# Issuing a 3.5 KB weight load from GpSimd three instructions earlier, ahead of the building of the head mask

## The chip, the cores and the metric

The kernel runs on one core of a Trainium2 chip. The metric is the device time of one execution in microseconds (us). The profile's span, from the first to the last instruction, is about 2.1 us shorter than the device time of the same execution. In the profile PE is TensorE's products, PEld its weight loads, DVE VectorE, ACT ScalarE, POOL GpSimd, and SPq, ACTq and POOLq are the queues on which SyncE, ScalarE and GpSimd issue transfers.

## The reference, cut to what matters

```python
# x [2048, 448], 16 heads of 28
qkv = x @ wqkv
pq = einsum("bhsd,hdf->bhsf", q, w_phi)      # a 28 x 28 matrix for each head
pk = einsum("bhsd,hdf->bhsf", k, w_phi)
phi = concat([softmax(p), softmax(-p)])      # for q and for k
# ... linear attention from phi_q, phi_k, v; output product with wo
b = gelu(x @ w1 + b1) @ w2 + b2
return g * a + (1 - g) * b                   # g = sigmoid(sum(x * gate_w))
```

The kernel multiplies the projections with w_phi once, ahead of everything that runs over tokens: Wpk = Wk times a block-diagonal matrix of the heads' w_phi, and Wpq in the same way. That block-diagonal matrix is what the moved load feeds.

## The kernel before

The parts that the argument touches. GpSimd builds an identity and a head mask, then issues the load of the last 64 rows of w_phi; ScalarE's queue loads the first 384.

```python
nc.scalar.dma_start(x0, x[0:512, :]...)                       # first block of x, 448 KB
nc.sync.dma_start(gate[0:1, :], gate_w[None, :])
for c, eng in ((0, nc.sync), (1, nc.scalar), (2, nc.sync)):   # WvG
    eng.dma_start(WvG[:, c, 0:D], A_wqkv[c * P:(c + 1) * P, 2 * D:3 * D])
nc.scalar.dma_start(WvG[64:P, 3, 0:D], ...)
nc.scalar.dma_start(wphi[:, 0:3, :], wphi_rows[0:384, :]...)  # the large w_phi load
# [cut]
load_wT(WkT, D)                                               # DMA transposes, SyncE
load_wT(WqT, 0)
# [cut]
nc.gpsimd.memset(ident[:], 1.0)
nc.gpsimd.affine_select(out=ident[:], ...)
nc.gpsimd.memset(hmask[:], 1.0)
nc.gpsimd.affine_select(out=hmask[:], ...)                    # twice
nc.gpsimd.dma_start(wphi[0:64, 3, :], wphi_rows[384:448, :])  # the small w_phi load
nc.gpsimd.memset(Wpq[0:HP, 3, :], 0.0)
# [cut: more clears on GpSimd]

def fill_bd():                                 # VectorE, four products, one for each chunk
    for c, (h0, h1) in enumerate(spans):
        nc.vector.tensor_tensor(out=bd[:, c, h0:h1, :], in0=wphi[:, c, ...],
                                in1=hmask[:, c, h0:h1, ...], op=ALU.mult)
# [cut]
dummies(7)            # TensorE: warm-up products
turn_x0(0, xp[0]); turn_gate(); turn_x0(1, xp[1])   # transposes of x on TensorE (L367)
fill_bd()
v_pair(0, on_act=True); v_pair(1)                   # 16 v products (L212)
prep(WkT, wk_at, (1, 0, 1)); prep(WqT, wq_at, (1, 0, 0))   # the weight products (L262)
swap_on_pool(WvS, WvG)                              # GpSimd copies (L400, L401), and others
# [cut: the k, q and v products over all tokens, the MLP, the output]
```

The softmax here doesn't subtract the row's maximum and nothing guards it: scores larger than these inputs give would overflow.

## Time and profile before

| | kernel before |
|---|---|
| device time, 3 runs | 149.19 us (149.14 to 149.22) |
| span of the profiled run | 147.5 us (that run: 149.62 us) |
| TensorE busy | 97% of the span |
| GpSimd busy | 46%, almost gapless to 12.5 us |
| the moved load | issued at 2.22 us, 0.76 us on GpSimd, landing after 4.2 us |

The lines of this profile are in the prediction, except one, the weight loads ahead of the second weight product, with their wait in brackets:

```profile
10.50 0.94 PEld L262 LDWEIGHTS <-WqT 128*128 128x128 bf16 x16 [0.46 <-DMA WqT<-in_A_wqkv_dram]
```

### The profile page before, as it was taken

How to read it: one execution, taken by the hardware profiler on the slowest of the kernel's cores; microseconds unless marked ns; L12 is line 12 of the kernel's file. 1: busy time of each engine (PE TensorE's matmuls, PEld its weight loads, DVE VectorE, ACT ScalarE, POOL GpSimd, SP SyncE). 2: the span in 40 equal slices, each digit the busy share in tenths (PEclk: the TensorE clock that was granted, in tenths of full speed). 3: DMA queues.
4: the chain of work that ended last, by engine and by line, in shares of the span. 5: the costliest groups of instructions: out<-in, count | busy, mean ns of one | idle time of the engine just before them, and what ended most of it. 6: DMA issues, size and time to landing. Idle time of an engine off the chain costs nothing.

```text
span 147.5 us, 3138 instructions
## 1 busy us (share of the span) xinstructions
PE 143.4 (97%) x1302; PEld 75.0 (51%) x1302; DVE 87.9 (60%) x139; ACT 75.2 (51%) x91; POOL 68.4 (46%) x49
## 2 busy tenths in 40 slices
PE   7999999999999999999999999999999999999992
PEld 2665544555544854444444445554555455555462
DVE  2353699999999999999300017765665245550312
ACT  1654999989889436767677774000621021111100
POOL 7999999899977999919950000000000000000000
PEclk9999999999999999999999999999999999999999
DMA  4999999999700089982999913333433012225011
GB/s 142 227 215 193 168 195 222 218 220 214 160 2 2 4 144 131 226 169 47 126 158 201 351 66 71 71 76 73 129 98 76 31 62 67 67 67 71 31 62 31
DMA packets 44928, 18.02 MB, mean 122 GB/s; under 512 B 36785, under 2 KB 44914, under 8 KB 44914
## 3 DMA queue, kind: packets, MB, share of 16 engines
q1 hardware_dynamic: 43698, 17.16, 56.5%
q10 hardware_dynamic: 1152, 0.65, 1.6%
q8 instruction: 10, 0.16, 0.5%
q14 instruction: 4, 0.03, 0.1%
q0 software_dynamic: 64, 0.01, 0.0%
HBM read 6.28 MB, written 1.84 MB: 55 GB/s over the span
## 4 chain that ended last, share of the span: by engine, by line
PE 91%; DMA 4%; SPq 2%; DVE 1%; issue 0%
PE y L515 29%; PE hp L463 29%; PE pq L346 7%; PE y L520 6%; DMA WqT<-in_A_wqkv_dram 4%; PE v_ps L330 4%; PE pk L338 4%; PE pk L231 3%; PE acc L353 3%; PE nm L476 3%; SPq L146 2%; PE v_ps L231 2%; PE y L525 1%; PE w_ps L262 1%; PE pk L218 1%; SPq L134 1%
## 5 line engine op out<-in xcount | busy, mean ns | idle before, releaser
L515 PE MATMUL y<-w_sb,gel 128*128 128x448 bf16 (+2 forms) x238 | 45.2, 342 | 0.0
L463 PE MATMUL hp<-xT,w_sb 64*128 64x512 bf16 x196 | 42.6, 376 | 0.0
L463 PE MATMUL hp<-xS,w_sb 64*128 64x512 bf16 x196 | 42.6, 376 | 0.0
L468 ACT ACTIVATE gel<-hp,b1T 128x1024 bf16<-128x1024 f32 x28 | 30.8, 1110 | 13.2 <-PE hp L463 13.2
L515 PEld LDWEIGHTS <-gel 128*128 128x128 bf16 x238 | 22.3, 98 | 20.0 <-issue 0.9
L538 ACT ACTIVATE b2u<-b_sb,ungate 128x448 f32<-128x448 bf16 x16 | 10.2, 666 | 40.8 <-DVE res L530 40.8
L463 PEld LDWEIGHTS <-w_sb 64*128 64x128 bf16 x392 | 19.0, 94 | 23.0
L306 POOL TENSOR_TENSOR phik<-phik,rec 128x1792 bf16<-128x1792 bf16 (+1 forms) x8 | 24.9, 3126 | 1.8 <-DVE rec L303 1.7
L480 DVE TENSOR_SCALAR den<-nm,einv 128x16 f32<-128x16 f32 x16 | 3.7, 230 | 27.9 <-PE nm L476 27.9
L530 DVE SCALAR_TENSOR_TENSOR res<-y,ungate,b2u 128x448 bf16<-128x448 f32 (+2 forms) x17 | 10.8, 653 | 15.4 <-PE y L525 10.1
L301 DVE TENSOR_REDUCE sums<-phik 128x64 f32<-128x1792 bf16 x8 | 16.0, 2000 | 3.2 <-ACT phik L292 3.2
L306 POOL TENSOR_TENSOR oT<-oT,rec 128x1792 bf16<-128x1792 bf16 x4 | 12.7, 3212 | 1.1 <-DVE rec L303 1.1
L520 PE MATMUL y<-wo_sb,oT 128*128 128x448 bf16 (+2 forms) x51 | 11.7, 341 | 0.0
L346 PE MATMUL pq<-Wpq,xT 64*128 64x448 bf16 x56 | 11.5, 349 | 0.0
L346 PE MATMUL pq<-WqS,xS 64*128 64x448 bf16 x56 | 11.4, 349 | 0.0
L306 POOL TENSOR_TENSOR w_sb<-w_sb,rec 128x1792 bf16<-128x1792 bf16 x3 | 9.6, 3212 | 3.0 <-DVE rec L303 3.0
L483 DVE TENSOR_TENSOR o_tok<-nm,den 128x448 bf16<-128x448 f32 x16 | 10.0, 624 | 0.6
L303 DVE RECIPROCAL rec<-sums 128x64 f32<-128x64 f32 x16 | 8.8, 553 | 1.4
L200 DVE CAST vaug<-v_ps 128x896 bf16<-128x896 f32 x7 | 7.5, 1071 | 2.0 <-PE v_ps L212 1.6
L291 ACT ACTIVATE phik<-pk 128x896 bf16<-128x896 f32 x8 | 7.6, 947 | 1.9 <-PE pk L220 1.9
L301 DVE TENSOR_REDUCE sums<-oT 128x64 f32<-128x1792 bf16 x4 | 7.9, 1981 | 0.0
L292 ACT ACTIVATE phik<-pk 128x896 bf16<-128x896 f32 x8 | 7.7, 958 | 0.0
(113 smaller groups left out, 173.6 us busy)
## 6 DMA issues: line engine op xcount, KB each, us to landing
w_sb<-in_B_w_dram SPq DMA_DIRECT2D x4, 784.0 KB, 11.5
out_dram<-res SPq DMA_DIRECT2D x15, 112.0 KB, 1.8
w_sb<-in_B_w_dram SPq DMA_DIRECT2D x2, 448.0 KB, 4.8
w_sb<-in_B_w_dram SPq DMA_DIRECT2D x2, 336.0 KB, 3.7
xS<-xT SPq DMA_DIRECT2D x2, 256.0 KB, 3.5
EqT<-in_A_x_dram ACTq DMA_DIRECT2D x1, 448.0 KB, 3.2
xS<-xT SPq DMA_DIRECT2D x2, 192.0 KB, 3.5
wo_sb<-in_A_wo_dram SPq DMA_DIRECT2D x1, 336.0 KB, 16.9
```

What stands on the lines that cost most here:

```text
L292: nc.scalar.activation(out=dst[:, :, :, 1, 0:PW], in_=src, func=ACT.Exp, scale=-1.0)
L301: nc.vector.reduce_sum(out=sums[:], in_=ph, axis=AX.X)
L303: nc.vector.reciprocal(out=rec[:], in_=sums[:])
L306: eng.tensor_tensor(out=ph[:, lo:hi], in0=ph[:, lo:hi], in1=rec[:, lo:hi, :, None].to_broadcast([P, hi - lo, 2, DH]), op=ALU.mult)
L346: nc.tensor.matmul(pq[:, i, 0:D], lhsT=x_half(i, k, h)[:, r * P:(r + 1) * P], rhs=w_half(Wpq, WqS, i, k), start=(k == 0), stop=(k == NK - 1))
L463: nc.tensor.matmul(hp[:, i, :], lhsT=w1_sb[i * HP:(i + 1) * HP, k, j * P:(j + 1) * P], rhs=x_half(i, k, h), start=(k == 0), stop=(k == NK ...
L468: nc.scalar.activation(out=gel[h][:, j, :], in_=hp[:].rearrange("p a b -> p (a b)"), func=ACT.Gelu_apprx_tanh, bias=b1T[:, j:j + 1])
L483: nc.vector.tensor_tensor(out=o_tok[:, t % 4, 0:D].rearrange("p (x h d) -> p x h d", x=NPR, h=2), in0=nmv[:, :, 0:PW].rearrange("p x (h d) ...
L515: nc.tensor.matmul(y, lhsT=gel[t // 8][:, j, (t % 8) * P:(t % 8 + 1) * P], rhs=w2_sb[:, j, cols], start=(opens and j == 0), stop=False)
L520: nc.tensor.matmul(y, lhsT=oT[:, c, t * P:(t + 1) * P], rhs=wo_sb[:, c, cols], start=False, stop=(closes and c == 2))
L530: nc.vector.scalar_tensor_tensor(out=res[:, cols], in0=y, scalar=ungate[:, t:t + 1], in1=b2u[t][:, cols], op0=ALU.mult, op1=ALU.add)
L538: nc.scalar.activation(out=b2u[t][:], in_=b2_sb[:], func=ACT.Copy, scale=ungate[:, t:t + 1])
```

## The change

Its intent is to bring the small load forward, since the idle time of VectorE in front of the block-diagonal matrix is put down to "wphi". Nothing else changes.

```diff
     nc.gpsimd.affine_select(out=ident[:], in_=ident[:], pattern=[[-1, P]],
                             compare_op=ALU.is_equal, fill=0.0, base=0, channel_multiplier=1)
+    nc.gpsimd.dma_start(wphi[0:64, 3, :], wphi_rows[384:448, :])
     nc.gpsimd.memset(hmask[:], 1.0)
     [cut: the two affine_select of hmask]
-    nc.gpsimd.dma_start(wphi[0:64, 3, :], wphi_rows[384:448, :])
     spans = [(0, 5), (4, 10), (9, 14), (13, 16)]
```

## The prediction

> **What bounds the kernel now.** I started with the page of the profiled execution, its busy shares and its chain of work that ended last.
>
> ```profile
> span 147.5 us, 3138 instructions
> ...
> PE 143.4 (97%) x1302; PEld 75.0 (51%) x1302; DVE 87.9 (60%) x139; ACT 75.2 (51%) x91; POOL 68.4 (46%) x49
> ...
> PE 91%; DMA 4%; SPq 2%; DVE 1%; issue 0%
> ```
>
> TensorE is busy 97% of the span and makes up 91% of the chain. GpSimd, the engine whose order changes, is busy 46% of the span and has no entry in the chain. The part that is not TensorE lies at the start, so I next took the chain in order of time. The columns are start in us, length in us, and what it was.
>
> ```profile
> 2.53 0.04 issue
> 2.58 2.37 SPq L146
> 4.94 0.05 issue
> 4.99 5.47 DMA WqT<-in_A_wqkv_dram
> 10.46 0.05 issue
> 10.51 1.10 PE w_ps L262 x16
> 11.61 2.27 PE pk L231 x12
> 13.88 0.29 PE pk L218
> ```
>
> The chain runs through the SyncE queue: it issues the DMA transpose for WkT (2.37 us), then the one for WqT at 4.99, which lands 5.47 us later, at 10.46. Then TensorE starts the second weight product at 10.51 and works without a gap to the end (the remaining pieces of the chain follow each other on TensorE to 144.8, then the last output). So a change in the first 10 us is worth something only if it moves the landing of WqT, and something ahead of TensorE's other work only if it comes later than its slack. The view of waits for TensorE says the same: over the whole kernel it waits 1.1 us for the zeroed warm-up tile and 0.3 us for WqT, and for nothing else that is listed.
>
> What the moved load feeds: the timeline of the first microseconds shows it, and the product that consumes it.
>
> ```profile
> 1.47 0.15 POOL L166 MEMSET hmask<- 128x64 bf16 x1
> 1.68 0.27 POOL L167 TENSOR_SCALAR_AFFINE_SELECT hmask<-hmask 128x64 bf16<-128x64 bf16 x1
> 2.02 0.25 POOL L169 TENSOR_SCALAR_AFFINE_SELECT hmask<-hmask 128x64 bf16<-128x64 bf16 x1
> 2.22 0.76 POOL L171 DMA_DIRECT2D wphi<-in_A_w_phi_dram  x1
> ...
> 6.85 0.92 DVE L191 TENSOR_TENSOR w_sb<-wphi,hmask 128x140 bf16<-128x140 bf16 x4 [0.99 <-DMA wphi<-in_A_w_phi_dram]
> ```
>
> VectorE builds the block-diagonal weights (called w_sb in the trace, bd in the code) from wphi and hmask in four instructions, and sat idle 0.99 us before the first, for a wphi load. There are two: the large one on ScalarE's queue (chunks 0 to 2) and the small one on GpSimd's (64 rows of chunk 3). The table of DMA issues tells which came last.
>
> ```profile
> wphi<-in_A_w_phi_dram ACTq DMA_DIRECT2D x1, 21.0 KB, 4.3
> wphi<-in_A_w_phi_dram POOLq DMA_DIRECT2D x1, 3.5 KB, 4.2
> ```
>
> The small load is issued at 2.22 and takes 4.2, so it lands at about 6.4. The large one is issued at 2.42 (timeline) and takes 4.3, so it lands at about 6.7. The first VectorE instruction multiplies chunk 0 and waits for the large load; only the fourth, which starts at 7.5 (the view of this tile gives the last start), reads the small one. The small load has 7.5 - 6.4 = 1.1 us to spare before its only reader, and it is not what the idle 0.99 us waited for.
>
> **What the Trainium skill says.** "DMA: Bandwidth & Descriptors", in "SWDGE vs HWDGE vs iDMA", says that a DMA issued from GpSimd has its descriptors written by software on that engine, into rings kept in SBUF. The trace agrees that issuing is not free there: this 64-row load holds GpSimd's queue for 0.76 us, the 14-row bias load later for 0.54 us. The same page, "Issuing engines are not separate DMA queues", says DMAs from all queues run on the same 16 engines and interleave. The trace shows GpSimd's queue with 64 packets in all and a share that rounds to 0.0% of the DMA engines' span, so as traffic it is negligible at either place. "SBUF — State Buffer", in the box on the "DVE blocks DMA" trap, says VectorE in a two-port mode can lock GpSimd out of the port it needs for descriptors. That is the only way I see for the new place to cost more: VectorE clears tiles from 0.90 to 2.19. In the kernel before, GpSimd's own memset and selects run beside these at 0.15 to 0.29 us each without a visible stall, but its descriptor writing begins at 2.22, after the last clear, so the trace before does not show this case either way.
>
> **The change part by part.** It removes and adds nothing. The order of instructions on TensorE, VectorE, ScalarE and SyncE is the same before and after, waits included; on GpSimd one DMA issue moves ahead of three instructions.
>
> - The small load: the three instructions it overtakes occupy GpSimd's stream from 1.47 to 2.22, so its issue moves up by 0.75 us, to about 1.47. It should land near 1.47 + 4.2 = 5.7 instead of 6.4. Its reader at 7.5 does not care. Gain on the path: 0.
> - The head mask: its three instructions start behind the 0.76 us issue, so hmask is complete at 2.27 + 0.76 = about 3.0 instead of 2.27. Its reader starts at 6.85, 3.8 us later. Loss on the path: 0.
> - GpSimd after that: the next instruction (the clear of Wpq) started at 2.97, behind 0.75 + 0.75 us of these four. The same four in another order add up to the same, so it should start at 2.97 again, within about 0.05 us for the switch between issuing and computing. Everything later on GpSimd keeps its time.
> - VectorE's build at 6.85 to 7.77 still waits for ScalarE's load at 6.7. And had it moved, nothing would follow: TensorE reaches its first use of the blocks at 8.93 to 9.12 (timeline), 1.2 us after they are complete, because it is busy with the first v products; and then waits for WqT at 10.46.
> - DMA traffic: 3.5 KB leave the window around 4.2 to 5.1 us and go to around 3.5 to 4.4 (from the packets' start times in the trace). Per packet record it is 16 data packets of 16 ns and 16 completions of 9 ns, 0.4 us of engine time over 16 engines: 0.025 us each. This sits at worst ahead of the x block that TensorE transposes at 4.09, and at best no longer ahead of WkT and WqT. Estimated from these: -0.03 to +0.03 us.
>
> The sum is 0 +- 0.05 us on 149.19.
>
> **The rivals.**
>
> 1. The head start reaches the end. The idle 0.99 us in front of VectorE's build reads as if it were for the moved load, since the profile names both loads wphi. If it were, the build could begin 0.7 us sooner. For it: only the name. Against it: the two landings (6.4 and 6.7), and WqT behind it; even a build that took no time would leave TensorE at WqT's landing. Time: 149.2 all the same; the most that taking away the wait for WqT gives is its 0.3 us, 148.9.
> 2. Descriptor writing collides with VectorE's clears. In the new place, 1.47 to 2.22, it lies beside the clears of WvG (1.52 to 1.95) and Wpk (1.95 to 2.19). If GpSimd could not write until 2.19, its stream would slip by up to 0.7 us. It is nearly gapless from 0.81 to 12.53 us, so the slip would travel to the copy of x that TensorE's k products need (12.78, 0.61 us long). That copy has 0.25 us of wait for a transpose ahead of it and ends at 13.39, some 0.4 us before TensorE gets to L218 at 13.81. So of 0.7 us about 0.05 could reach TensorE, and the copies of WqS have 0.7 us to spare as well (19.04 against 19.77). Time: 149.2 to 149.3; 149.6 only if the slip is twice that. A clear is one output and no input, so I give a stall as such one chance in five.
> 3. Rearranged DMA traffic moves WqT's landing. All 16 engines are busy at 90% or more in most slices from 2.5 to 12 us, so the order of packets can matter more than their size. For it: the transposes are the path. Against it: SyncE issues them back to back (2.58 to 7.60), and its order and waits are unchanged. If the landing shifted by 0.2 us either way, the time would be 149.0 to 149.4.
>
> **The range and the chances.** The three runs of the kernel before lie within 149.14 to 149.22, so repetition alone gives 0.1 us. I add 0.2 us either way for rival 3, and a little above for rival 2 and for another chip: 148.9 to 149.5, centred on 149.2. A change of 2% is 3.0 us; no path here gives a third of that: the whole of TensorE's waiting is 1.4 us. So within 2% gets 0.97, and the rest is split evenly.
>
> **What would show each step right or wrong.** In the changed kernel's timeline: the small load's issue at about 1.5 us and 0.75 us long (over 1 us, with hmask's clear late, would be rival 2); hmask complete by about 3.0; the clear of Wpq at about 3.0; VectorE's build still at about 6.85, still waiting for a wphi load although the small one landed at about 5.7; TensorE's first use of the blocks still at about 9.1; the landing of WqT within 0.2 us of 10.46, and the span within 0.3 us of 147.5. A build that starts at 6.1 would show that I took the wrong load for the last one; a WqT landing half a microsecond away would show rival 3. The prediction as a whole is wrong if the time leaves 148.9 to 149.5, most likely by the transposes' landing.

## The result, and the profile after

| | before, same rounds | changed |
|---|---|---|
| device time, 4 runs each | 149.20 us (149.14 to 149.24) | 149.16 us (149.03 to 149.31) |
| ratio | | 0.9998, 95% interval 0.998 to 1.0015 |

A ratio is the mean time of one kernel's fast runs over that of the other's fast runs of the same rounds, so it isn't quite the ratio of the medians.

The page of the changed kernel (its span, and the chain that ended last by engine):

```profile
span 147.0 us, 3138 instructions
...
PE 97%; DVE 1%; issue 0%
```

The span is 0.59 us shorter than in the profile of before (147.54 and 146.96), though the medians of the times are equal, and the DMA that had 4% of the chain is gone from it. The chain in order of time (start, length, what) shows what has taken its place:

```profile
1.06 3.17 PE warm_ps L384 x7
4.23 0.92 PE xp L367 x8
...
5.17 0.70 DVE xT L200
...
5.92 3.22 PE v_ps L212 x16
9.14 1.89 PE w_ps L262 x32
11.03 2.27 PE pk L231 x12
```

TensorE goes from its warm-up products through the transposes of x and the v products into the weight products, and no wait for WqT shows. It was close: WqT, issued at 5.00, landed at 9.86, and the first product that reads it started at 9.90. In the profile of before TensorE waited for that landing until 10.46. The timeline of GpSimd and VectorE shows the moved instruction and its reader:

```profile
1.49 0.76 POOL L166 DMA_DIRECT2D wphi<-in_A_w_phi_dram  x1
...
2.25 0.18 POOL L167 MEMSET hmask<- 128x64 bf16 x1
...
2.83 0.25 POOL L170 TENSOR_SCALAR_AFFINE_SELECT hmask<-hmask 128x64 bf16<-128x64 bf16 x1
3.03 0.46 POOL L173 MEMSET Wpq<- 64x448 bf16 x1
...
6.01 0.96 DVE L191 TENSOR_TENSOR w_sb<-wphi,hmask 128x140 bf16<-128x140 bf16 x4
```

The issue moved from 2.22 to 1.49 and is as long as before, the mask is complete at 3.08, and the clear of Wpq starts 0.06 us later than before. VectorE's build starts at 6.01, 0.84 us sooner than in the profile of before. The table of DMA issues (last column: us from issue to landing) says why:

```profile
wphi<-in_A_w_phi_dram ACTq DMA_DIRECT2D x1, 21.0 KB, 3.5
...
wphi<-in_A_w_phi_dram POOLq DMA_DIRECT2D x1, 3.5 KB, 3.5
```

Both w_phi loads are faster than in the profile of before, the large one too, which the change doesn't touch (4.3 before). So the two profiles differ in things that the diff doesn't explain. Are these differences the change's doing, lost again elsewhere, or are they of the single run? That was the first question for the chip.

### The profile page after: what moved, and what is told of

It reads as the page before. It is cut to its first block, busy times and chain, and to the rows that moved or that the text cites. A ratio compares the mean times of both kernels' runs of the same rounds, so it can differ in the third digit from the quotient of the medians.

```text
span 147.0 us, 3138 instructions
## 1 busy us (share of the span) xinstructions
PE 142.9 (97%) x1302; PEld 74.5 (51%) x1302; DVE 87.9 (60%) x139; ACT 75.2 (51%) x91; POOL 68.4 (47%) x49
## 3 DMA queue, kind: packets, MB, share of 16 engines
HBM read 6.28 MB, written 1.84 MB: 55 GB/s over the span
## 4 chain that ended last, share of the span: by engine, by line
PE 97%; DVE 1%; issue 0%
PE y L515 29%; PE hp L463 29%; PE pq L346 7%; PE y L520 6%; PE v_ps L330 4%; PE pk L338 4%; PE pk L231 3%; PE acc L353 3%; PE nm L476 3%; PE v_ps L212 2%; PE warm_ps L384 2%; PE v_ps L231 2%; PE w_ps L262 1%; PE y L525 1%; PE xp L367 1%; PE pk L218 1%
```

## The experiments

Theory: the position of this load is worth nothing, and what differs between the two profiles differs from run to run. Rival: the earlier load brings the other transfers, and with them WqT, forward by half a microsecond. Eleven runs were made, in three calls; the kernels of one call ran on the same chip and share the runs of the kernel before (medians 149.39, 149.10 and 149.31 us).

### Both kernels again, twice each

No edit.

> The kernel before, unchanged, a second time. Theory: the landing of the WqT transpose and the end of TensorE's slow start differ from run to run, whatever the kernel, so the 0.5 us between the two first profiles (147.5 and 147.0) is such a difference. Then the ratio of this kernel to before is 1.000 with an interval of about 0.1 to 0.2%, and its WqT may land anywhere from 9.6 to 10.6. Rival (the moved load brings WqT forward): WqT lands at 10.4 to 10.5 again, the span is 147.5 again.

> The changed kernel a second time, timed on the same chip as the repeat of before. Theory: ratio 1.000, within 0.1%; WqT anywhere from 9.6 to 10.6. Rival: WqT lands at 9.9 or sooner again, span 147.0 again, and the ratio is 0.997 or lower.

> A third profile of the kernel before. Theory: the landings of WqT in the profiles of before and of the changed kernel overlap. Rival: all those of before lie at least 0.3 us later than all those of the changed kernel.

> A third profile of the changed kernel. Theory: as for the third profile of before, the landings overlap; GpSimd's issue at 1.5 and the clear of Wpq at 3.0 repeat to 0.05 us. Rival: WqT at 9.9 or sooner in all three.

Measured: before_rep1 149.22 us (148.90 to 149.50, 6 runs), ratio 0.9988 (0.9969 to 1.0007); after_rep1 149.29 us (148.99 to 149.41, 6 runs), ratio 0.9993 (0.9977 to 1.0009); before_rep2 149.17 and after_rep2 149.68 us, one run each. All six profiles together (the last column is from the trace's record of the granted clock: the moment from which TensorE has its full clock):

| profile | device us | span us | w_phi landings, small / large: us from issue | WqT issue + landing | v products, us | build starts | full clock from |
|---|---|---|---|---|---|---|---|
| before | 149.62 | 147.5 | 4.2 / 4.3 | 4.99 + 5.5 | 3.37 | 6.85 | 6.26 |
| before_rep1 | 149.47 | 147.4 | 3.6 / 3.6 | 4.90 + 4.8 | 3.60 | 6.17 | 6.78 |
| before_rep2 | 149.17 | 147.1 | 3.7 / 3.8 | 4.92 + 5.1 | 3.27 | 6.29 | 6.01 |
| changed | 149.03 | 147.0 | 3.5 / 3.5 | 5.00 + 4.9 | 3.22 | 6.01 | 5.09 |
| after_rep1 | 149.36 | 147.3 | 3.8 / 3.7 | 5.01 + 5.0 | 3.55 | 6.28 | 6.63 |
| after_rep2 | 149.68 | 147.6 | 3.5 / 3.6 | 4.98 + 5.0 | 3.67 | 6.16 | 7.05 |

The repeats of before land WqT at 9.7 and 10.0, those of the changed kernel at 10.0 and 9.9: they overlap, and the rival falls. The list of waits shows a wait of TensorE for WqT only in the first profile of before (0.46 us ahead of its weight loads); in the other five the chain is 97% TensorE. But before_rep2 has a shorter one that no list shows: WqT landed at 9.99, its first product started at 10.04, 0.17 us after the product ahead of it instead of 0.04, and the weight products took 2.00 us instead of 1.89. In the changed kernel's first profile the two came together, and in the other three WqT was 0.3 to 0.6 us early. So two chains of nearly equal length, the landing of WqT and TensorE's own stream, meet at the weight products, and the later one sets the start. With the waits for WqT (0.46 and 0.11 us) taken off, the span follows the column of the v products: span less wait less v products is 143.7 to 143.8 us in five profiles, and 143.9 in after_rep2, whose v products began 0.17 us later than those of the changed kernel's first profile (6.09 and 5.92). Here is the chain in order of time in before_rep1, in before_rep2 (one line) and in after_rep2:

```profile
4.23 0.93 PE xp L367 x8
...
6.12 3.43 PE v_ps L212 x16
9.55 1.89 PE w_ps L262 x32
```

```profile
9.14 2.00 PE w_ps L262 x32
```

```profile
4.27 1.03 PE xp L367 x8
...
6.26 3.50 PE v_ps L212 x16
9.76 1.89 PE w_ps L262 x32
```

In the changed kernel's first profile the v products ended at 9.14 instead of 9.55 and 9.76. The gaps between the starts of TensorE's products in the trace show the reason: it begins at a slow pace (107 ns from one 128-column transpose to the next, 374 ns for a 449-column v product) and at some moment goes over to twice that (55 and 190 ns). In the changed kernel's first profile the eight transposes from 5.08 on are already fast; in after_rep2 the first three v products are still slow and the pace doubles after 7.0 us. The other four lie between, and the record of the clock (last column) puts the six in the same order as the v products. The Trainium skill describes this: "TensorE: Matmul & The Clock Gate", section "Part 1: The HAM clock gate", says that TensorE runs at half its clock until an activity window that does not start with the kernel has seen it busy. The traces agree on the two paces and on the moment changing from run to run.

### The load later instead of earlier

```diff
# late_a
-    nc.gpsimd.dma_start(wphi[0:64, 3, :], wphi_rows[384:448, :])
     nc.gpsimd.memset(Wpq...); nc.gpsimd.memset(vaug...); nc.gpsimd.memset(phik...)
+    nc.gpsimd.dma_start(wphi[0:64, 3, :], wphi_rows[384:448, :])
# late_b: the same, behind the last clear (o_tok)
```

> The small load moved the other way, behind three clears, so that GpSimd issues it at about 4.7 instead of 2.2. With the 3.5 to 4.2 us seen from issue to landing it lands at 8.3 to 9.0, and the last of VectorE's four products ends by 9.3 at the latest, about when TensorE asks for it (9.2 to 9.5). Theory (the load has a second or more to spare): within 0.1 us of before, ratio 0.999 to 1.001. Rival (the start waits for this load, so that 2.5 us later costs something like it): at least 1 us slower, ratio 1.007 or more.

> The small load behind all of GpSimd's clears, issued at about 7.2, landing at 10.8 to 11.3. Now it should come last: TensorE waits for the fourth product from about 9.4 to 11.1 to 11.6. Theory: 1.5 to 2.1 us slower, 150.8 to 151.4, ratio 1.010 to 1.014; the two delays show where the slack ends. If it costs less than 0.5 us, TensorE's stream has more slack at the weight product than the traces show.

late_a: 149.15 us (149.07 to 149.24) against 149.10, ratio 1.0007 (0.9992 to 1.0022). The load was issued at 4.64, 2.4 us later than in before, and landed at 8.24, 1.8 to 2.5 us later than in the three profiles of before. That cost nothing, as the theory said. The timeline of VectorE and GpSimd in late_a:

```profile
8.34 0.25 DVE L191 TENSOR_TENSOR w_sb<-wphi,hmask 128x84 bf16<-128x84 bf16 x1 [1.43 <-DMA wphi<-in_A_w_phi_dram]
...
8.69 1.68 POOL L400 COPY WvS<-WvG 64x1796 bf16<-64x1796 bf16 x1
```

VectorE's fourth product waits 1.43 us for the load, in brackets, and ends at 8.59, in time for TensorE, which starts the weight products at 9.01. (TensorE then waited 0.2 us for WqT, which landed at 10.08: the other chain again.)

late_b: 151.56, 151.56, 152.82 and 153.23 us, ratio 1.0234 (1.0181 to 1.0287), beyond the 151.4 expected at most. The profile is of a run of 151.56 us. GpSimd, VectorE and TensorE in it:

```profile
10.27 1.31 POOL L401 COPY WvS<-WvG 64x1347 bf16<-64x1347 bf16 x1
...
11.11 0.56 DVE L191 TENSOR_TENSOR w_sb<-wphi,hmask 128x84 bf16<-128x84 bf16 x1 [3.50 <-DMA wphi<-in_A_w_phi_dram]
...
11.73 0.89 PE L262 MATMUL w_ps<-w_sb,WkT 128*128 128x84 bf16 x13 [2.31 <-DVE w_sb L191]
```

Here TensorE waits 2.31 us for VectorE's fourth product. That accounts for most of the 2.46 us by which the faster pair of runs is above 149.10. The slower pair is another 1.3 to 1.7 us longer and has no profile, but its mean granted clock is 0.989 against 1.0 of the faster pair, as in the two pairs of pad_6 below, where a profile shows what such a run looks like. The same product took 0.56 us instead of 0.25 while GpSimd copied; more on this below.

So the load's slack ends somewhere between a landing at 8.24 and one at 11.02. Before and changed land it at 5.0 to 6.4: both are on the flat part, which is why the change is worth nothing.

### How much delay on GpSimd is free

```diff
     nc.gpsimd.memset(Wpq[0:HP, 3, :], 0.0)
+    nc.gpsimd.memset(Wpq[0:HP, 3, :], 0.0)   # pad_2: two more; pad_6: six more
```

> Kernel before with the clear of Wpq done three times instead of once: two more instructions at 0.41 us, about 0.8 us of delay for everything later on GpSimd. It measures GpSimd's slack, which the second rival of the prediction rested on (0.65 us there). Theory: 0.1 to 0.4 us slower, ratio 1.001 to 1.003. If GpSimd were on the path: 0.8 us slower, 1.005. If its slack were over 1 us: 1.000.

> The same with six more clears, about 2.5 us of delay on GpSimd. Theory: 1.7 to 2.2 us slower (2.5 less a slack of 0.3 to 0.8), ratio 1.011 to 1.015. If GpSimd's slack were over 2 us: under 1.003.

pad_2: 149.89 us (149.82 to 149.93), ratio 1.0056 (1.0041 to 1.0071): 0.79 us more than 149.10, where I expected 0.1 to 0.4. The timeline of GpSimd tells why, and the view of TensorE's waits (what it waited for; us in total, times, longest) shows where it arrives (two lines were added, so L220 is L218 of before):

```profile
12.92 0.40 POOL L409 COPY EqT<-xT 64x256 bf16<-64x256 bf16 x1
```

```profile
PE pk L220 <- POOL WkS L410: 0.6, 1, 0.6
```

The first copy started at 11.63 in before, so two clears delayed GpSimd by 1.29 us and not 0.8: back to back they start 0.52 to 0.56 us apart, and the selects beside them got longer too. Of 1.29 us, 1.29 - 0.79 = 0.50 us was free. pad_6 confirms it: the copy starts at 14.80, a delay of 3.17 us, and the faster two runs (151.75 and 151.76) are 2.65 us above 149.10, so 0.52 us was free. Its ratio of 1.0238 (1.0178 to 1.0298) mixes these with two runs of 153.41 and 153.46. One of those was profiled:

```profile
16.89 4.11 PE L237 MATMUL pk<-Wpk,xT 128*128 128x448 bf16 x12
```

These twelve k products took 2.44 us in before (there on L231). TensorE had just waited 2.1 us for GpSimd, and was back at its slow pace for most of them: the trace's record gives it half the clock from 16.88 to 20.30 us. Half of these 3.4 us is 1.7 us, which is the distance between the two pairs of runs. A wait of TensorE of this length can thus cost 1.7 us more than itself in some runs and nothing more in others. The change under study moved GpSimd's later work by 0.06 us, one eighth of the 0.50 us that is free.

### Does the landing of WqT set the end?

```diff
# gate_after
-    nc.sync.dma_start(gate[0:1, :], gate_w[None, :])
     for c, eng in ((0, nc.sync), (1, nc.scalar), (2, nc.sync)):
         eng.dma_start(WvG[:, c, 0:D], A_wqkv[c * P:(c + 1) * P, 2 * D:3 * D])
+    nc.sync.dma_start(gate[0:1, :], gate_w[None, :])
```

> Kernel before with the gate row's load behind the two WvG loads on SyncE's queue. SyncE now waits for VectorE's clears before its first load; with WvG first it can start some 0.4 us sooner, and the WkT and WqT transposes with it. It tests whether the landing of WqT sets the end, as the prediction read the first profile. By the repeats it does not (TensorE had no wait for WqT in four of five later profiles): within 0.15 us of before, ratio 0.999 to 1.001. As the prediction read it: 0.3 to 0.5 us faster, ratio 0.9970 to 0.9980.

Measured: 152.10 us (151.69 to 152.23, 6 runs), ratio 1.0183 (1.0164 to 1.0201). This fits neither expectation, so it settles nothing about WqT: SyncE started WkT at 2.11 instead of 2.58, but WqT only at 5.39 instead of 4.99. It shows something else. The table of DMA issues, then VectorE and GpSimd in the timeline:

```profile
EqT<-in_A_x_dram ACTq DMA_DIRECT2D x1, 448.0 KB, 4.6
```

```profile
8.25 3.54 DVE L191 TENSOR_TENSOR w_sb<-wphi,hmask 128x140 bf16<-128x140 bf16 x4 [1.48 <-DMA wphi<-in_A_w_phi_dram]
...
8.54 1.80 POOL L400 COPY WvS<-WvG 64x1796 bf16<-64x1796 bf16 x1
10.39 1.31 POOL L401 COPY WvS<-WvG 64x1347 bf16<-64x1347 bf16 x1
```

The block of x that TensorE transposes first (into EqT) lands after 4.6 us instead of 3.2, as SyncE's loads now run beside it from the start, and the large w_phi load after 5.7 instead of 4.3. So VectorE's build starts at 8.25, and now it takes 3.54 us instead of 0.92. It ends at 11.79, just as GpSimd's two copies end (11.70), and TensorE starts the last product of its first group only at 11.85. The four products one by one: two that began before the copies took 0.31 and 0.33 us, the third ended at 10.50, 0.16 us behind the end of the first copy, and the fourth 0.09 us behind the end of the second. The Trainium skill has a cause that fits: "SBUF — State Buffer", section "SBUF: two separate sides", says that VectorE and GpSimd share one pair of ports as an exclusive lock, which also a VectorE operation with two SBUF inputs needs against a GpSimd operation that reads SBUF. Three traces here agree: this one, late_b's 0.56 us, and the next run's. In before and changed the build is over by 7.8 us, ahead of the copies at 8.5, and pays nothing.

### The load away from GpSimd

```diff
     nc.scalar.dma_start(wphi[:, 0:3, :], wphi_rows[0:384, :]...)
+    nc.scalar.dma_start(wphi[0:64, 3, :], wphi_rows[384:448, :])
     [cut]
-    nc.gpsimd.dma_start(wphi[0:64, 3, :], wphi_rows[384:448, :])
```

> The small load taken from GpSimd's queue altogether and issued by ScalarE after the large one. GpSimd's later work moves up by about 0.75 us, the load lands at about 6.5. Theory: neither matters, within 0.15 us of before, ratio 0.999 to 1.001. If GpSimd's stream, or the interplay of its descriptor writing with other transfers, held the start: 0.3 us faster or more.

Measured: 149.75 us (149.46 to 149.85) against 149.31, ratio 1.002 (0.9998 to 1.0041). The interval just includes no difference; the median is 0.44 us above. The expectation that it would not matter is not clearly refuted, but the trace shows two things that went against the edit. ScalarE and its queue first, then GpSimd beside VectorE:

```profile
4.13 0.47 ACTq L137 DMA_DIRECT2D wphi<-in_A_w_phi_dram  x1
4.64 1.28 ACT L163 ACT_TABLE_LOAD   x1 [4.64 <-DMA EqT<-in_A_x_dram]
```

```profile
7.94 1.67 POOL L400 COPY WvS<-WvG 64x1796 bf16<-64x1796 bf16 x1
...
8.15 1.57 DVE L191 TENSOR_TENSOR w_sb<-wphi,hmask 128x84 bf16<-128x84 bf16 x1 [1.17 <-DMA wphi<-in_A_w_phi_dram]
```

The added load on ScalarE's queue starts only at 4.13, right after the x block issued ahead of it has landed (4.11), and not at about 3.0; why the built program waits for it is not shown. The table load behind it starts at 4.64 instead of 3.05, and the first gate columns that the v products read are ready only at about 6.2, so these start at 6.28 instead of 5.91, a delay of the size of the 0.44 us. And since GpSimd is 0.6 us ahead, its copy meets VectorE's fourth product, which takes 1.57 us instead of 0.25 and ends at 9.72, right behind the copy's end at 9.61. That did not reach TensorE, whose weight products (9.62 to 11.67) have no gap. So freeing GpSimd of its 0.76 us gained nothing here; whether this version is slower than before stays open.

### Is it the slow pace of TensorE that sets the start?

```diff
-    dummies(7)
+    dummies(1)
```

> Kernel before with 1 of the 7 warm-up products, so that TensorE is idle from about 1.5 to 4.1. It tests whether the moment at which TensorE's pace doubles follows from earlier work and sets the start. Theory: the pace doubles up to 2.6 us later than the 5 to 7 us seen, so most of the 16 v products run at 374 ns instead of 190: 1.0 to 3.0 us slower, ratio 1.007 to 1.020. If the moment is independent of TensorE's work: within 0.3 us of before.

Measured: 150.50 us (149.99 to 150.76), ratio 1.0072 (1.0049 to 1.0096), at the lower end of the theory's range. In the timeline the 16 v products are

```profile
5.91 4.96 PE L212 MATMUL v_ps<-WvG,xT 128*128 128x449 bf16 x16
```

against 3.2 to 3.7 us in the six profiles above; the gaps between their starts are 353 to 378 ns up to 9.3 us and 190 ns from 9.6 us on. The moment depends on TensorE's own earlier work, and a later moment costs time one for one where no wait hides it: TensorE was back at its k products at 12.59 against 11.44 in the first profile of before, 1.15 us later, and the times of these two profiled runs differ by 150.76 - 149.62 = 1.14 us (the medians by 1.19). The v products took 1.59 us longer; the rest of that had been hidden in before by its wait for WqT.

No experiment points to a version that beats both kernels.

## Why the prediction was right or wrong

The time (149.16 us for 149.2), the range and "within 2%" were right. The steps, in the prediction's order:

1. **What bounds the kernel: this step failed.** The prediction put it as "a change in the first 10 us is worth something only if it moves the landing of WqT". That holds for the profiled execution (a wait of 0.46 us) and hardly or not at all for the other five: before_rep2 waited 0.11 us, the rest not measurably. There the start is TensorE's own stream from its first warm-up product at 1.06 us, and its length varies with the moment at which its pace doubles; cold_1 moved that moment and with it the time. I had read one execution, the slowest but one of the six, as the kernel, and missed a second chain that ends within 0.6 us of the first. The conclusion survived since the small load lies on neither.
2. **The ceiling of 0.3 us was mis-sized.** The wait for WqT was taken from the list of TensorE's product waits. The profile of the changed kernel, without that wait, has a span 0.59 us shorter: the weight loads had waited 0.46 us, and the v products of that run were another 0.15 us longer. Nor is the whole waiting of 1.4 us less than a third of 3.0 us, as the paragraph on the range has it; but 1.1 us of it is the wait for the warm-up tile, which the change doesn't touch.
3. **Small load at 1.47, 0.75 us long; mask at 3.0; clear of Wpq at 3.0:** right, with 1.49, 0.76, 3.08 and 3.03, in all three profiles to 0.02 us.
4. **Landing at 5.7:** it landed at 1.49 + 3.5 = 5.0 (5.0 and 5.3 in the repeats). The 4.2 us was of one run; the repeats of before have 3.6 and 3.7.
5. **VectorE's build still at 6.85: wrong**, it started at 6.01 to 6.28, and so it did in the repeats of before (6.17 and 6.29). It follows the large load, as the prediction said: it starts 0.10 us after that load's landing in all six profiles, and the landing was late in the first one (6.75, against 5.9 to 6.2). By its own sign, "a build that starts at 6.1", the prediction would have taken the wrong load for the last; that sign misleads. Rival 1, that the idle time belonged to the moved load, has nothing for it: in the changed kernel that load landed 1.0 us before the build began, and in late_a a landing 1.8 to 2.5 us later cost nothing.
6. **"1.1 us to spare before its only reader":** true, but the wrong measure. The limit is TensorE's first weight product at about 9.0 to 9.6 and GpSimd's copy at 8.5, which locks VectorE out. By late_a and late_b the true slack is over 1.8 us (8.24 - 6.4).
7. **Rival 2, descriptor writing against VectorE's clears:** it did not happen, 0.76 us in both places. Its slack of 0.65 us for GpSimd measured 0.50 to 0.52 by pad_2 and pad_6. That slack is small, and delays beyond it cost one for one.
8. **Rival 3, transfers rearranged:** landings of WqT do move, by up to 0.75 us (9.7 to 10.46), but between runs of the same kernel. By the prediction's own signs (WqT within 0.2 us of 10.46, the span within 0.3 us of 147.5) the first profile of the changed kernel, with 9.86 and 147.0, spoke for this rival; only the repeats of before, with 9.7 and 10.0, took that away. No effect of the change shows in six profiles. An effect of under about 0.2% of the time (what the intervals leave) stays open.

## What to carry to other kernels

Before you move a transfer, ask what its reader waits for last, and how late the transfer could be without cost; pushing it later on purpose, until it costs, measures that slack better than pulling it forward. Take at least two more profiles of the unchanged kernel before you build on a wait of some tenths of a microsecond: here half a microsecond of difference between two profiles belonged to the runs. And ask of a chain how far behind it the next one ends. Operations of VectorE with two inputs should be over before GpSimd begins long copies; here they ended with the copies otherwise.

## What the Trainium skill lacked or had wrong

- "TensorE: Matmul & The Clock Gate", Part 1, gives the moment of doubling a run-to-run variation of 500 ns either way, though it also calls the number of slow products run-variable. Here the moment spread over 3 us: late_b and gate_after were fast from their first transpose (4.0 and 5.4 us), the changed kernel's first profile from about 5.0, and after_rep2 only after 7.0 us, all with seven warm-up products from 1.06 us on. Together with the wait for WqT it accounts for the spans of the six profiles, 147.0 to 147.6 us.
- The same page says TensorE returns to the slow pace after about 3.4 us of idleness. In pad_6 it was slow again after a wait of 2.1 us in the profiled run: the clock fell to half at 16.88, 1.1 us after the wait had ended, and for 3.4 us. Two of four runs (153.41 and 153.46 against 151.75 us) were slower by as much as these twelve slow products account for.
- "SBUF — State Buffer" has the lock between VectorE's two-input operations and GpSimd's reads right, but gives no durations for such a pair. Here a product of 0.25 us took 1.57 us and ended 0.1 us behind GpSimd's copy, and four of 0.92 us took 3.54 us, two of them ending 0.1 to 0.2 us behind a copy.
- No page that I read says how far the time from issue to landing of an unchanged load varies: the 21 KB load took 3.5 to 4.3 us in the six profiles, and 5.7 us when two other loads were issued 0.9 us sooner.
- On the descriptor writing of a GpSimd DMA beside VectorE's clears there is no figure either: 0.76 us for 64 rows, beside them and after them.
